# Moving table work between engines in the opening stage of a fused Fourier-mixing and maxout kernel

## The chip, the core and the metric

The kernel runs on one core of one Trainium2 chip. The metric is device time in microseconds of one execution; the figure for a kernel is the median of its runs. The core has a matrix engine (PE, with weight loads PEld), a vector engine (DVE), a scalar engine (ACT), GpSimd (POOL) and SyncE (SP), each with its own in-order queue. POOL and SP issue the transfers (DMA) here.

## The reference

For 8 batches of 3072 tokens by 256 features, the real part of a two-dimensional Fourier transform, then a feed-forward layer that takes the largest of three products:

```python
X = np.fft.fft(x, axis=1)          # x: (8, 3072, 256)
X = np.fft.fft(X, axis=2)
x = X.real.reshape(8 * 3072, 256)
h = np.maximum(np.maximum(x @ w1, x @ w2), x @ w3)   # w1, w2, w3: (256, 768)
out = h @ w_out                                      # w_out: (768, 256)
```

## The kernel before

**What it computes.** The transform along the tokens is done in two stages per batch (class `Mix`). Rows `a*96 + s` are loaded with `a` on partitions and `s` along the free dimension, the second 32 partitions holding the mirrored `s` (`load_x`); `mirror` copies features 255 to 129 into partitions 64 to 127, so that sums and differences of a pair come out of one product. Stage one (`s`, seven pieces) multiplies with a 32-point table `tab` and evicts into `tb`; for batch 0 a single DVE instruction, `t`, transposes `tb` into `yb` (later batches go through DRAM). Stage two (`k(which, g)`) multiplies `yb` with the tables `te_tab` (which 0) or `to_tab` (which 1), in three groups g of 512 columns, and evicts into `tE` and `tO`. The transform along the features is folded into the weights: `product` forms, for w2 and for w3, the feature transform times that weight less w1; `keep` evicts these banks into `g_all`, and `differ` makes `gd_all` from `g_all` for the mirrored tokens. What all three products share goes through `g1t` and `gw` straight to the output.

**Units.** A batch has 18 units: three blocks of 512 tokens by six chunks of 128 hidden columns. A unit's `begin` makes two sums on PE (four matmuls) and takes their maximum into `hp` (ACT writes `stmp`, DVE takes the maximum); its `finish` adds two matmuls with `gd_all` into the same banks and takes `hm` likewise. On PE the order is begin(g), finish(g-1), then what `plan` holds for that unit. The first bank of unit g is that of unit g-2, the second one too for even units, so a begin waits for ACT's `stmp` and DVE's `hm` of unit g-2. The last of the six chunks of a block is followed by the output products of that block (`l2_block`).

**The head.** All tables are made on the chip during batch 0's first two stages. For the stage-two tables POOL writes ramps into `kvec` (`ramp`, three iotas and three small ones). For each group of columns, `phase` turns the ramp into a phase (times `s_of`, plus `phi`, per partition), `turns` rounds it to whole turns by adding and taking away a large constant (two ACT operations into `q`), `wrap` takes the whole turns off (DVE), and `table(0)`, `table(1)`, `table(2)` write te_tab (sine), q (absolute value) and to_tab (sine of what is left), all on ACT. The feature tables `md_all` and `nmd_all` come from `vm` in the same way, with a period of 256. The third group's phase, turns and wrap are `angle(0)` and `angle(1)`, four DVE operations in units 1 and 2.

**Order.** The program's order is written by hand: every engine runs its instructions in the order in which the Python code issues them. Batch 0's x comes in four parts (`FIRST`, eight transfers issued by POOL), each followed by its `mirror`, DVE's for the block and ACT's for the first column (the fourth part's by DVE). `warm_up(n)` puts n matmuls on zeros where PE would else stand still. PSUM has three banks in `ps_f`, which banks of `product`, `k`, `g1t` and others pass through in turn; the five banks of `ps_s` serve stage one and then the units.

Lines of the profile that the change and the prediction speak of: L127 x loads, L134 and L138 mirrors, L150 iotas, L175 weight loads, L219 and L223 DVE or POOL arithmetic with scalars, L261 and L262 turns, L299 to L303 tables, L311 products, L325 keep, L332 differ, L341 g_all by `prep_first`, L371 g1t by `prep_second`, L405 and L413 stage-one evictions, L431 the transpose, L463 and L465 stage two and its evictions, L487, L488 and L494 unit matmuls, L500 stmp, L501 hp and hm, L637 warm-ups, L823 POOL's sums of later units.

Of the kernel before, what the change touches and what calls it, by code (L numbers as in the profile page):

```python
# [9 lines left out]
FP32 = mybir.dt.float32  # L10
# [3 lines left out]
AX = mybir.ActivationFunctionType  # L14
ALU = mybir.AluOpType
# [36 lines left out]
def kernel(  # L52
# [96 lines left out]
    def iota(t, pattern, base=0, cm=0):  # L149
        nc.gpsimd.iota(t, pattern, base=base, channel_multiplier=cm,  # L150
                       allow_small_or_imprecise_dtypes=True)
# [12 lines left out]
    for i in range(2):  # L164
        nc.vector.memset(xt[i][32:64, 0::48, :], 0.0)
    for c, (s0, s1) in enumerate(FIRST):
        for h in range(2):
            load_x(0, s0, s1, h)
        if c == 0:
            dvec = gen.tile([128, 128], FP32, tag="dvec")  # L170
            iota(dvec, [[1, 128]])

# [6 lines left out]
    kvec = gen.tile([128, NHALF + 1], FP32, tag="kvec")  # L179
    kv = kvec[:, 0:1440].rearrange("p (r j) -> p r j", j=96)  # L180

    def ramp(r):
        n = {0: 6, 6: 5, 11: 4}[r]
        iota(kv[:, r:r + n, :], [[1, n], [32, 96]], base=r + 1)

    load_w(0, 0, 128)
    ramp(0)
    load_w(1, 0, 128)
    ramp(6)
    load_w(2, 0, 128)  # L190
# [23 lines left out]
    def small(name):  # L214
        return gen.tile([128, 1], FP32, name=name, tag=name)
# [14 lines left out]
    scal(hflag, sidx, 32.0, ALU.is_ge)  # L230
    scal(alpha, sidx, -2.0, ALU.mult, 31.0, ALU.add)
# [27 lines left out]
    def turns(q, v, per):  # L259

        nc.scalar.activation(out=q, in_=v, func=AX.Identity, scale=1.0 / per, bias=rnd[:, 0:1])  # L261
        nc.scalar.activation(out=q, in_=q, func=AX.Identity, scale=1.0, bias=rnd[:, 1:2])  # L262

    turns(qm, vm, 256.0)
    phi, s_of = small("phi"), small("s_of")
    scal(phi, hflag, -768.0, ALU.mult, 1536.0, ALU.add)
    mad(s_of, hflag, -32.0, sidx)
    mad(s_of, s_of, 2.0, up)
    mirror(0, *FIRST[0])
# [3 lines left out]
    def phase(c0, c1):  # L273
        scal(kvec[:, c0:c1], kvec[:, c0:c1], s_of, ALU.mult, phi, ALU.add)
# [5 lines left out]
    turns(q[:, 0:512], kvec[:, 0:512], 3072.0)  # L280
    mad(vm, qm, -256.0, vm)
    nc.vector.tensor_copy(out=vm.rearrange("p (fc k c) -> p fc k c", fc=2, k=2)[:, :, :, 0],
                          in_=par.unsqueeze(1).to_broadcast([128, 2, 2]))
    phase(512, 1024)
    mirror(0, *FIRST[1])

    def angle(part, c0=1024, c1=NHALF + 1):
        cs = slice(c0, c1)
        if part == 0:
            phase(c0, c1)  # L290
            scal(q[:, cs], kvec[:, cs], 1.0 / 3072.0, ALU.mult, ROUND, ALU.add)
        else:
            scal(q[:, cs], q[:, cs], -ROUND, ALU.add, -3072.0, ALU.mult)
            nc.vector.tensor_tensor(out=kvec[:, cs], in0=kvec[:, cs], in1=q[:, cs], op=ALU.add)
# [65 lines left out]
    def prep_second():  # L360

        for jp in range(NJC // 2):
# [8 lines left out]
            nc.vector.tensor_copy(out=g1t[:, jp * 512:(jp + 1) * 512], in_=pst)  # L371
# [269 lines left out]
    m.s(0, pool=ps_s)  # L641
    m.s(1, pool=ps_s)
    warm_up(4)
    wrap(0, 512)
    mirror(0, *FIRST[2])
    nc.scalar.activation(out=md_all, in_=vm, func=AX.Sin, scale=float(2.0 * math.pi / 256.0))
    m.s(2, pool=ps_s)
    m.s(3, pool=ps_s, evict=dve)
# [6 lines left out]
    m.s(5, pool=ps_s)  # L655
    m.s(6, pool=ps_s, evict=dve)
# [3 lines left out]
    table(0, 0, 512)  # L660
# [3 lines left out]
    qs = q[:, 512:1024]  # L664
    scal(qs, kvec[:, 512:1024], 1.0 / 3072.0, ALU.mult, ROUND, ALU.add, eng=nc.gpsimd)
    scal(qs, qs, -ROUND, ALU.add, eng=nc.gpsimd)
    HALVES = ((0, 25), (25, NS))
    for (s0, s1) in HALVES:
        for h in range(2):
            load_x(1, s0, s1, h)  # L670
        if s0 == 0:
            nc.gpsimd.dma_start(out=wout_bf.rearrange("p (jc c) -> p jc c", jc=NJC),
                                in_=moe_w_out.rearrange("(jc p) c -> p jc c", jc=NJC))
    psg0 = products(ps_f, 0, 2, 0, 128)
    keep(psg0, 0, 2, 0, 128, nc.scalar.copy)
    table(1, 0, 512)
# [4 lines left out]
    warm_up(3)  # L681
    m.c(1, 7)
    m.k(0, 0, dve)
    m.k(1, 0)
    psg2 = products(ps_f, 1, 2, 128, 384)
    wrap(512, 1024)
    scal(dif, sgn, 1.0, ALU.subtract)
    differ(0, 2, 0, 128)
    keep(psg2, 1, 2, 128, 384, dve)
    table(1, 512, 1024)  # L690
    differ(0, 2, 128, 384)
    m.f()

    rows_f = gen.tile([128, 12 * B], FP32, tag="rows_f")
    iota(rows_f.rearrange("p (b t u) -> p b t u", t=4, u=3), [[S, B], [-4, 4], [-1025, 3]],
         base=S - 1, cm=-32)
    rows_v = rows_f.rearrange("p (b r) -> p b r", r=12)
    adj = gen.tile([128, 12], FP32, tag="adj")
    adv = adj.rearrange("p (t u) -> p t u", u=3)
    four = pidx.to_broadcast([128, 4])  # L700
    pool = nc.gpsimd
    for u in range(3):
        scal(adv[:, :, u], four, float(96 - 32 * u), ALU.is_ge, 3071.0, ALU.mult, eng=pool)
    low = gen.tile([128, 2], FP32, tag="low")
    scal(low[:, 0:1], pidx, 47.0, ALU.is_ge, 1520.0, ALU.mult, eng=pool)
    scal(low[:, 1:2], pidx, 95.0, ALU.is_ge, -511.0, ALU.mult, eng=pool)
    scal(low[:, 0:1], low[:, 0:1], 2031.0, ALU.add, eng=pool)
    pool.tensor_tensor(out=adj[:, 11:12], in0=low[:, 0:1], in1=low[:, 1:2], op=ALU.add)
    pool.tensor_tensor(out=rows_v, in0=rows_v,
                       in1=adj.unsqueeze(1).to_broadcast([128, B, 12]), op=ALU.add)  # L710
    pool.tensor_copy(rows_m, rows_f)
# [52 lines left out]
    for (u, fn) in ((0, lambda: table(2, 512, 1024)), (0, lambda: m.c(7, 16)),  # L764
                    (0, lambda: next(second)), (0, lambda: next(first)),
                    (1, lambda: m.k(1, 1)), (1, lambda: next(second)), (1, lambda: next(first)),
                    (1, lambda: table(0, 512, 1024)), (1, lambda: angle(0)),
# [152 lines left out]
```

## Time and profile before

| | |
|---|---|
| median of 3 runs | 400.74 us (398.99 to 402.38) |
| the profiled execution | 398.77 us, of which the span 396.9 |
| granted PE clock, mean over the span | 0.999 |
| PE busy, 0 to 10 us | 7.63 us |
| PE busy, 10 to 20 us | 6.30 us |
| PE busy, 20 to 30 us | 9.95 us |
| PE busy, 30 to 40 us | 7.77 us |
| PE busy, 40 to 50 us | 9.13 us |

The profile is one execution. Its span begins with the first instruction and ends with the last; the execution's own time is 1.9 us longer. A timeline row reads: start in us, duration in us, engine, source line, operation, what it writes and reads, partitions by elements and type, how often in a row, and in brackets how long the engine had been idle before it and what ended that. A row with xN stands for N equal instructions in a row, and its duration is from the first one's start to the last one's end. Consecutive instructions of one engine overlap by up to a tenth of a microsecond, so durations add up to a little more than the time they take. PE's busy time counts the warm-ups on zeros.

### The profile page before, as it was taken

What the parts mean: (1) busy time and instruction counts of PE and PEld (TensorE: products, weight loads), DVE (VectorE), ACT (ScalarE), POOL (GpSimd) and SP (SyncE); (2) the same over time, 40 slices, a digit from 0 to 9 for tenths busy, and PEclk for the clock granted to TensorE, in tenths of its full rate; (3) what the DMA queues carried; (4) which work ended last, traced back from release to release, by engine and by line L of the source; (5) the groups of instructions that cost most, each with busy time, mean ns of one, the idle gap of its engine ahead of it and who ended that gap; (6) DMA issues with size and microseconds to landing.
All of it is one profiled execution on the core that took longest, in us unless ns stands there. A gap on an engine that the chain in (4) does not pass through costs nothing.

```text
span 396.9 us, 8384 instructions
## 1 busy us (share of the span) xinstructions
PE 379.8 (96%) x2712; PEld 236.5 (60%) x2761; DVE 319.0 (80%) x534; ACT 261.9 (66%) x474; POOL 331.9 (84%) x430
## 2 busy tenths in 40 slices
PE   7697999999999999999999999999999999999994
PEld 2264566656665666656665666656665666666673
DVE  7897797887887887877887887877887887887982
ACT  3876789678767787578866788568766547444420
POOL 9983588879988899889988899889967898869993
PEclk9999999999999999999999999999999999999999
DMA  8999476494666876495666767395333553321234
GB/s 119 160 181 167 96 195 152 115 208 131 138 153 114 194 159 153 114 211 125 137 157 124 192 135 170 107 192 146 115 107 89 138 144 94 88 82 47 89 94 132
DMA packets 66901, 54.20 MB, mean 137 GB/s; under 512 B 32702, under 2 KB 62556, under 8 KB 66003
## 3 DMA queue, kind: packets, MB, share of 16 engines
q0 software_dynamic: 24368, 26.53, 35.2%
q1 hardware_dynamic: 41978, 26.72, 26.9%
q8 instruction: 21, 0.34, 0.4%
q10 hardware_dynamic: 512, 0.43, 0.3%
q14 instruction: 22, 0.18, 0.1%
HBM read 36.95 MB, written 30.81 MB: 171 GB/s over the span
## 4 chain that ended last, share of the span: by engine, by line
PE 83%; DVE 7%; ACT 4%; issue 3%; POOL 1%; DVEq 0%; POOLq 0%; ACTq 0%
PE po L510 30%; PE pse L494 12%; PE pse L487 8%; PE pse L488 6%; PE po L533 5%; PE pse L830 4%; PE d L816 3%; PE e L814 3%; PE pse L831 3%; PE ps L398 3%; PE ps L463 2%; PE pl L525 2%; ACT tb L402 1%; DVE yb L431 1%; ACT stmp L500 1%
## 5 line engine op out<-in xcount | busy, mean ns | idle before, releaser
L500 ACT ACTIVATE stmp<-pse 128x512 bf16<-128x512 f32 x150 | 89.5, 600 | 63.7 <-PE pse L494 50.3
L823 POOL TENSOR_TENSOR plus<-even,odd 128x512 bf16<-128x512 f32 x69 | 87.9, 1274 | 38.0 <-DVE even L819 27.8
L619 POOL DMA_INDIRECT out_dram<-ot,rows_m x92 | 102.5, 1114 | 17.8 <-issue 10.5
L823 POOL TENSOR_TENSOR minus<-even,odd 128x512 bf16<-128x512 f32 x69 | 87.7, 1270 | 0.0
L510 PE MATMUL po<-wout_bf,hp 128*128 128x256 bf16 x576 | 86.1, 273 | 0.4
L832 DVE SCALAR_TENSOR_TENSOR hp<-pse,plus 128x512 bf16<-128x512 f32 x69 | 47.6, 689 | 45.2 <-POOL plus L823 15.6
L510 PE MATMUL po<-wout_bf,hm 128*128 128x256 bf16 x576 | 78.6, 273 | 0.0
L510 PEld LDWEIGHTS <-hp 128*128 128x128 bf16 x576 | 56.4, 98 | 26.1
L494 PE MATMUL pse<-tO,gd_all 128*128 128x512 bf16 x218 | 70.8, 379 | 1.0
L510 PEld LDWEIGHTS <-hm 128*128 128x128 bf16 x576 | 56.4, 98 | 16.3
L538 DVE TENSOR_TENSOR ot<-po,even 128x512 f32<-128x512 f32 x92 | 62.7, 681 | 0.0
L487 PE MATMUL pse<-tE,g_all 128*128 128x512 bf16 x149 | 56.4, 379 | 3.3 <-DVE hm L501 1.6
L501 DVE TENSOR_TENSOR hp<-pse,stmp 128x512 bf16<-128x512 f32 x75 | 51.3, 684 | 9.4 <-ACT stmp L500 8.6
L501 DVE TENSOR_TENSOR hm<-pse,stmp 128x512 bf16<-128x512 f32 x75 | 51.5, 687 | 8.2 <-ACT stmp L500 3.5
L819 DVE SCALAR_TENSOR_TENSOR even<-vb,wcol,e 128x512 f32<-128x512 bf16 x69 | 50.9, 737 | 0.0
L488 PE MATMUL pse<-tO,g_all 128*128 128x512 bf16 x129 | 48.9, 379 | 0.1
L844 DVE SCALAR_TENSOR_TENSOR hm<-pse,minus 128x512 bf16<-128x512 f32 x69 | 47.1, 682 | 1.3 <-PE pse L488 0.7
L818 ACT ACTIVATE odd<-d 128x512 f32<-128x512 f32 x69 | 41.3, 599 | 6.4 <-issue 0.4
L134 ACT COPY xt<-xt 64x762 bf16<-64x762 bf16 (+1 forms) x48 | 40.2, 838 | 1.1
L494 PEld LDWEIGHTS <-gd_all 128*128 128x128 bf16 x219 | 21.3, 97 | 23.0 <-issue 5.0
L533 PE MATMUL po<-gw,tO 128*128 128x512 bf16 x85 | 32.3, 380 | 0.0
L402 ACT CAST tb<-ps 128x512 bf16<-128x512 f32 x40 | 21.6, 589 | 14.8 <-PE ps L398 14.0
(175 smaller groups left out, 478.0 us busy)
## 6 DMA issues: line engine op xcount, KB each, us to landing
xt<-in_x_dram POOLq DMA_DIRECT2D x14, 384.0 KB
out_dram<-ot SPq DMA_DIRECT2D x55, 96.0 KB
out_dram<-ot SPq DMA_DIRECT2D x64, 64.0 KB
db<-tb SPq DMA_DIRECT2D x21, 192.0 KB
vb<-vd SPq DMA_DIRECT2D x23, 128.0 KB
xt<-in_x_dram POOLq DMA_DIRECT2D x7, 400.0 KB
xt<-in_x_dram POOLq DMA_DIRECT2D x7, 368.0 KB
out_dram<-ot SPq DMA_DIRECT2D x62, 32.0 KB
```

The source lines that it names most:

```text
L487: nc.tensor.matmul(pse[:, 0:n], g_all[:, jc, 2 * i, :], te, start=True, stop=False)
L488: nc.tensor.matmul(pse[:, 0:n], g_all[:, jc, 2 * i + 1, :], to, start=False, stop=True)
L494: nc.tensor.matmul(pse, gd_all[:, jc, i, :], to, start=False, stop=True, skip_group_check=True)
L500: nc.scalar.activation(out=stmp[:, 0:n], in_=pses[0][:, 0:n], func=AX.Relu)
L501: nc.vector.tensor_tensor(out=dst, in0=src3, in1=stmp[:, 0:n], op=ALU.max)
L510: nc.tensor.matmul(po, hcols(jc), wout_bf[:, jc * 256:(jc + 1) * 256], start=False, stop=(jc == NJC - 1), skip_group_check=True)
L533: nc.tensor.matmul(po, to[:, cp], gw[:, 256:768], start=True, stop=True)
L538: nc.vector.tensor_tensor(out=ot.rearrange("p (h c) -> p h c", h=2), in0=po.rearrange("p (h c) -> p h c", h=2), in1=lin.unsqueeze(1).to_br ...
L619: stored(nc.gpsimd.indirect_dma_start(out, bass.IndirectOffsetOnAxis(ap=rows_m[0:128 - lo, at_row: at_row + 1], axis=0), ot[lo:128, 256:51 ...
L819: nc.vector.scalar_tensor_tensor(out=even3, in0=vb, scalar=wcol[:, jc:jc + 1], in1=e3, op0=ALU.mult, op1=ALU.add)
L823: nc.gpsimd.tensor_tensor(out=dst, in0=even3, in1=odd3, op=op)
L832: nc.vector.scalar_tensor_tensor(out=dst, in0=pse2, scalar=0.0, in1=sums[g][0], op0=ALU.max, op1=ALU.max)
```

## The change

What moves, by engine:

- POOL: the ramps of the first two groups go from between the first weight loads to between the parts of x. The two operations on `q` of the second group ahead of batch 1's loads go. `angle`, all four operations for the third group, comes to POOL behind `m.f`; the sums for the scatter indices (`rows`) go from there to unit 5.
- ACT: takes `phase` for two groups and `turns` for the second one; gives `turns` of vm to DVE. It evicts s3 and s6 of stage one, which DVE evicted, and DVE evicts s5, which ACT evicted. `md_all` comes two evictions later, `table(0)` and `table(1)` of early groups come earlier, the third group's `table(1)` moves from unit 3 to unit 2, and one of three g1t evictions comes from DVE.
- DVE: loses two phases, a product of vm, the third group's four operations, one eviction of g1t; takes the three operations of `_reduce` for vm; `wrap` of the second group moves ahead of the third mirror, `dif` ahead of the transpose.
- PE: the fourth product bank (psg2, eight matmuls) goes from behind stage two's first two pieces to ahead of them, and two warm-ups fewer stand there.

```diff
+    def ramp(r):
...
     for c, (s0, s1) in enumerate(FIRST):
         for h in range(2):
             load_x(0, s0, s1, h)
         if c == 0:
-            dvec = gen.tile([128, 128], FP32, tag="dvec")
             iota(dvec, [[1, 128]])
+        elif c < 3:
+            ramp((0, 6)[c - 1])
...
-    load_w(0, 0, 128)
-    ramp(0)
-    load_w(1, 0, 128)
-    ramp(6)
-    load_w(2, 0, 128)
+    for k in range(3):
+        load_w(k, 0, 128)
...
-    turns(qm, vm, 256.0)
...
     def phase(c0, c1):
-        scal(kvec[:, c0:c1], kvec[:, c0:c1], s_of, ALU.mult, phi, ALU.add)
+        nc.scalar.activation(out=kvec[:, c0:c1], in_=kvec[:, c0:c1], func=AX.Identity,
+                             scale=s_of, bias=phi)
...
     phase(0, 512)
-    turns(q[:, 0:512], kvec[:, 0:512], 3072.0)
-    mad(vm, qm, -256.0, vm)
+    turns(0, 512)
+    phase(512, 1024)
+    mirror(0, *FIRST[0])
+    turns(512, 1024)
+    _reduce(nc, vm, vm, qm, 256.0)
     nc.vector.tensor_copy(out=vm.rearrange("p (fc k c) -> p fc k c", fc=2, k=2)[:, :, :, 0],
                           in_=par.unsqueeze(1).to_broadcast([128, 2, 2]))
-    phase(512, 1024)
-    mirror(0, *FIRST[1])
+    wrap(0, 512)
...
+    def angle(c0=1024, c1=NHALF + 1):
+        v, t, pool = kvec[:, c0:c1], q[:, c0:c1], nc.gpsimd
+        scal(v, v, s_of, ALU.mult, phi, ALU.add, eng=pool)
+        scal(t, v, 1.0 / 3072.0, ALU.mult, ROUND, ALU.add, eng=pool)
+        scal(t, t, -ROUND, ALU.add, -3072.0, ALU.mult, eng=pool)
+        pool.tensor_tensor(out=v, in0=v, in1=t, op=ALU.add)
...
-            nc.vector.tensor_copy(out=g1t[:, jp * 512:(jp + 1) * 512], in_=pst)
+            (nc.scalar.copy if jp == 2 else nc.vector.tensor_copy)(
+                out=g1t[:, jp * 512:(jp + 1) * 512], in_=pst)
...
     m.s(0, pool=ps_s)
+    mirror(0, *FIRST[1])
     m.s(1, pool=ps_s)
     warm_up(4)
-    wrap(0, 512)
+    table(0, 0, 512)
+    wrap(512, 1024)
     mirror(0, *FIRST[2])
-    nc.scalar.activation(out=md_all, in_=vm, func=AX.Sin, scale=float(2.0 * math.pi / 256.0))
     m.s(2, pool=ps_s)
-    m.s(3, pool=ps_s, evict=dve)
+    m.s(3, pool=ps_s)
+    nc.scalar.activation(out=md_all, in_=vm, func=AX.Sin, scale=float(2.0 * math.pi / 256.0))
...
-    m.s(5, pool=ps_s)
-    m.s(6, pool=ps_s, evict=dve)
+    scal(dif, sgn, 1.0, ALU.subtract)
+    m.s(5, pool=ps_s, evict=dve)
+    m.s(6, pool=ps_s)
     m.t()
     warm_up(2)
     nc.scalar.activation(out=nmd_all, in_=vm, func=AX.Sin, scale=float(-2.0 * math.pi / 256.0))
-    table(0, 0, 512)
...
-    qs = q[:, 512:1024]
-    scal(qs, kvec[:, 512:1024], 1.0 / 3072.0, ALU.mult, ROUND, ALU.add, eng=nc.gpsimd)
-    scal(qs, qs, -ROUND, ALU.add, eng=nc.gpsimd)
...
     psg0 = products(ps_f, 0, 2, 0, 128)
+    table(1, 0, 512)
     keep(psg0, 0, 2, 0, 128, nc.scalar.copy)
-    table(1, 0, 512)
     table(2, 0, 512)
     psg1 = products(ps_f, 0, 1, 128, 384)
     m.x0(x0s)
     keep(psg1, 0, 1, 128, 384, nc.scalar.copy)
-    warm_up(3)
+    psg2 = products(ps_f, 1, 2, 128, 384)
+    table(1, 512, 1024)
     m.c(1, 7)
+    warm_up(1)
     m.k(0, 0, dve)
     m.k(1, 0)
-    psg2 = products(ps_f, 1, 2, 128, 384)
-    wrap(512, 1024)
-    scal(dif, sgn, 1.0, ALU.subtract)
     differ(0, 2, 0, 128)
     keep(psg2, 1, 2, 128, 384, dve)
-    table(1, 512, 1024)
     differ(0, 2, 128, 384)
     m.f()
+    angle()
+
+    def rows():
...
-                    (1, lambda: table(0, 512, 1024)), (1, lambda: angle(0)),
+                    (1, lambda: table(0, 512, 1024)),
...
-                    (2, lambda: next(second)), (2, lambda: next(first)), (2, lambda: angle(1)),
+                    (2, lambda: next(second)), (2, lambda: next(first)), (2, lambda: table(1)),
                     (3, lambda: m.c(16, RI)), (3, lambda: m.c(0, 1)),
-                    (3, lambda: table(1)), (3, lambda: table(2)), (3, lambda: table(0)),
+                    (3, lambda: table(2)), (3, lambda: table(0)), (5, rows),
```

The lines of `rows` are those that stood behind `m.f` before, now in a function. `phi` and `s_of` are computed a little earlier on DVE.

## The prediction

> **What bounds the kernel now.** I read the page first (busy time, slices), then busy time by stage, then the head engine by engine in order of time.
>
> ```profile
> span 396.9 us, 8384 instructions
> PE 379.8 (96%) x2712; PEld 236.5 (60%) x2761; DVE 319.0 (80%) x534; ACT 261.9 (66%) x474; POOL 331.9 (84%) x430
> ```
> ```profile
> 0.00:19.90 19.90, 13.83 (x69) 5.67 (x70) 16.79 (x54) 12.14 (x24) 18.65 (x40) 1.00 1.00 139
> 19.90:36.43 16.53, 14.25 (x111) 8.37 (x114) 14.03 (x26) 12.77 (x28) 12.73 (x28) 1.00 1.10 168
> 45.00:390.00 345.00, 341.95 (x2453) 216.43 (x2496) 280.78 (x441) 231.17 (x411) 297.76 (x360) 1.00 0.59 135
> ```
>
> The last three rows are stretches: length, then busy us of PE, PEld, DVE, ACT, POOL, then PE clock and DMA. From 45 to 390 us PE is busy 341.95 of 345: that part runs at PE's pace and keeps its length, whatever happens in the head. So the change, which moves nothing behind unit 5 of batch 0, is worth what it takes off the start of that PE-bound run. In the head PE waits: 2.28 of the 16.53 us after 19.9, and before 19.9 much of its work is warm-up on zeros.
>
> Who it waits for, by the timeline:
>
> ```profile
> 7.66 0.81 DVE L134 COPY xt<-xt 64x2032 bf16<-64x2032 bf16 x1
> 8.49 0.99 DVE L219 TENSOR_SCALAR kvec<-kvec,s_of,phi 128x512 f32<-128x512 f32 x1
> 9.41 0.67 DVE L223 SCALAR_TENSOR_TENSOR vm<-qm,vm 128x512 f32<-128x512 f32 x1
> 10.12 0.60 DVE L282 COPY vm<-par 128x4 f32<-128x4 f32 x1
> 10.19 0.78 DVE L219 TENSOR_SCALAR kvec<-kvec,s_of,phi 128x512 f32<-128x512 f32 x1
> ...
> 13.16 0.69 DVE L405 CAST tb<-ps 128x512 bf16<-128x512 f32 x1
> 13.87 0.48 DVE L134 COPY xt<-xt 64x1143 bf16<-64x1143 bf16 x1
> ...
> 16.07 3.78 DVE L431 STREAM_TRANSPOSE yb<-tb 128x2048 uint32<-128x2048 uint32 x1 [0.52 <-ACT tb L405]
> 20.34 0.69 DVE L465 CAST tE<-ps 128x512 bf16<-128x512 f32 x1 [0.50 <-PE ps L463]
> 20.95 0.68 DVE L223 SCALAR_TENSOR_TENSOR kvec<-q,kvec 128x512 f32<-128x512 f32 x1
> ```
> ```profile
> 15.14 0.59 ACT L405 CAST tb<-ps 128x512 bf16<-128x512 f32 x1 [0.88 <-PE ps L408]
> ```
> ```profile
> 21.33 0.38 PE L487 MATMUL pse<-tE,g_all 128*128 128x512 bf16 x1
> 31.27 0.38 PE L487 MATMUL pse<-tE,g_all 128*128 128x512 bf16 x1 [0.47 <-ACT stmp L500]
> 33.42 0.38 PE L487 MATMUL pse<-tE,g_all 128*128 128x512 bf16 x1 [1.56 <-DVE hm L501]
> 35.14 0.81 PE L487 MATMUL pse<-tE,g_all 128*128 128x512 bf16 x2
> ```
>
> DVE has no gap from 7.66 to the fourth mirror at 13.87. That mirror releases the last stage-one matmuls, ACT evicts one of them until 15.73, and 0.34 later the transpose starts; stage two follows it. After the transpose DVE is again without a gap until about 33.4, and PE's largest stall (1.56, at 33.42) ends on DVE's hm. Two DVE queues in a row, then, set when PE's even run begins.
>
> **Part 1: up to the transpose.** From DVE's queue between 7.66 and 13.87 the change takes the two phases (0.99 and 0.78), the product of vm (0.67) and the eviction of s3 (0.69): 3.13. It puts in vm's whole reduction (three operations) and the second wrap, which moves here. The nearest rows of these:
>
> ```profile
> 27.58 0.43 DVE L219 TENSOR_SCALAR q<-kvec 128x513 f32<-128x513 f32 x1
> 31.04 0.41 DVE L219 TENSOR_SCALAR q<-q 128x513 f32<-128x513 f32 x1
> 31.48 0.70 DVE L294 TENSOR_TENSOR kvec<-kvec,q 128x513 f32<-128x513 f32 x1
> ```
>
> Reduction 0.43 + 0.41 + 0.70 = 1.54, wrap 0.68, in all 2.22: DVE could reach the fourth mirror at 13.87 - 0.91 = 12.96. But the data must be there. No view gives its landing; the packets do:
>
> ```profile
> DMA packets 333, 0.09 MB, mean 172 GB/s; under 512 B 310, under 2 KB 333, under 8 KB 333
> ```
>
> That is 12.0 to 12.5 us: 310 of 333 packets are already the short ones of the first weight loads, which stand behind x in the queue, so nearly all of x is through; 13.87 is the upper bound, since the mirror started without waiting. I take 13.25, near the lower end: 0.62 gained. The two ramps now stand between x's issues:
>
> ```profile
> 3.10 3.35 POOL L127 DMA_DIRECT2D xt<-in_x_dram  x6
> 7.14 0.73 POOL L150 IOTA kvec<- 128x576 f32 x1
> 8.62 0.58 POOL L150 IOTA kvec<- 128x480 f32 x1
> ```
>
> They push the issue of the fourth part 0.73 + 0.58 = 1.31 later, to end at 7.76. I cost that at nothing, because the transfers lag the issues by some 6 us (issued by 6.45, through after 12) and are fed from a backlog; if they followed the issue one for one, landing would be up to 1.31 later and this part's gain gone (rival 2). From there the chain is as before but for the last eviction, now DVE's at 0.69 instead of ACT's at 0.59: +0.10. Gain of part 1: 0.62 - 0.10 = 0.52, say **0.5**; bounds 0.8 (landing never waited for) and 0 (the reduction held up by POOL by 0.6, as the 128x4 copy at 10.12 shows such a hold). ACT takes two phases and four turns (six at 0.72, 4.3 us) from about 5.2 us on, where it now waits for DVE; its evictions of s2 and s3, the table md, s4 and s6 (four at 0.54 from start to start, 0.28) then need 2.4 us from 12.1 and end before DVE's eviction of s5 (14.5 to 15.2). The new transpose start is 16.07 - 0.5 = 15.57, its end 19.35.
>
> **Part 2: the first unit.** The fourth product bank (eight matmuls, 0.88) leaves the place between stage two and unit 0 and goes under the transpose:
>
> ```profile
> 18.25 0.59 PE L637 MATMUL warm<-zero 128*128 128x512 bf16 x2
> 20.45 0.38 PE L311 MATMUL psg<-w_bf,md_all 128*128 128x256 bf16 x2
> ```
>
> Cover: PE has only warm-ups from 18.25 to 19.90; 18.25 + 0.88 is 19.1, and one warm-up of 0.2 still fits. Unit 0 then starts as soon as tE is evicted: that took 20.34 + 0.69 - 19.85 = 1.18 after the transpose, against 21.33 - 19.85 = 1.48 before. Gain **0.3** (0 to 0.3); the rest of the 0.88 becomes slack on PE, which is not the late one here.
>
> **Part 3: units 0 to 5.** DVE loses the wrap (0.68), the third group's four operations (0.68 by the row below, 0.43, 0.41, 0.70) and one g1t (0.68): 3.6 us of the 13 between 20.3 and 33.4.
>
> ```profile
> 26.87 0.68 DVE L219 TENSOR_SCALAR kvec<-kvec,s_of,phi 128x513 f32<-128x513 f32 x1
> 29.59 0.68 DVE L371 CAST g1t<-pst 128x512 bf16<-128x512 f32 x1
> 29.44 0.48 ACT L341 CAST g_all<-psg 128x384 bf16<-128x384 f32 x1 [0.90 <-PE psg L311]
> 29.88 1.34 ACT L500 ACTIVATE stmp<-pse 128x512 bf16<-128x512 f32 x2
> 32.21 0.63 ACT L301 ACTIVATE q<-kvec 128x513 f32<-128x513 f32 x1 [0.82 <-DVE kvec L294]
> ```
>
> What is late next is ACT. It gains that g1t (0.59) and does the third group's Abs (0.63) ahead of unit 3's two stmp instead of behind them. Of this g1t fits ACT's idle time before 29.44 (0.9), Abs does not. Counted from the transpose's end: unit 3's stmp at 10.35 and 10.9 to 11.5 (before, 29.88 - 19.85 = 10.03 and to 11.4), hm behind it to 12.3, so unit 4's second pair starts at 12.3 against 33.42 - 19.85 = 13.57. Then ACT does the last two tables (0.65 and 0.55 from start to start) and two stmp (0.53 each), and unit 5 starts at 14.1 against 35.14 - 19.85 = 15.29: **1.2** less, the 0.3 of part 2 in it. From there PE's work is the same.
>
> POOL: angle is four operations. The rows nearest to them:
>
> ```profile
> 16.60 0.62 POOL L219 TENSOR_SCALAR q<-kvec 128x512 f32<-128x512 f32 x1
> 17.31 1.52 POOL L219 TENSOR_SCALAR q<-q 128x512 f32<-128x512 f32 x1
> 43.35 1.27 POOL L823 TENSOR_TENSOR plus<-even,odd 128x512 bf16<-128x512 f32 x1 [9.64 <-ACT tb L402]
> ```
>
> Three at 0.62 and one at 1.27 make 3.1, four at 1.52 make 6.1. With the first two rows' 2.1 us gone ahead of batch 1's loads, POOL is free when the transpose ends; m.f's copies and memsets (1.7 us) come first, so angle starts at about 21.4 and ends between 24.5 and 27.5; ACT asks for it at 19.35 + 9.8 = 29.1. It is hidden as long as it takes under 7.7 us; beyond that each us costs one. The loads of batch 1 go out 2 us earlier, and the index sums (3.7 us) end by 37.5, ahead of the first plus at 43.35 and of any scatter: nothing.
>
> **The sum.** 0.5 + 1.2 = 1.7. The profiled execution took 398.77 us (span 396.9 and 1.9 around it): 397.1 after. The median of the runs shown is 400.74, 2 above it: 400.74 - 1.7 = **399.0**.
>
> **Rivals.**
> 1. More comes off. The transpose's 3.78 lies beside POOL's 0.62 and 1.52; one of like form takes 2.5 times the other. If that 0.9 is mutual hindrance, the transpose loses 0.9 as well: 2.6 off, 398.1. For it: the two rows; against: the first of the two ran under the same transpose and was short. 0.13.
> 2. Nothing to speak of comes off. The load sets the fourth mirror (part 1 gives 0) and ACT is held by g1t and Abs together (1.2 less 0.6 to 1.2): 0 to 0.6 off, 400.4. 0.17.
> 3. Slower: POOL's angle holds up DVE. One row shows how:
>
> ```profile
> 26.60 0.34 DVE L332 TENSOR_SCALAR gd_all<-g_all,dif 128x384 bf16<-128x384 bf16 x1
> 29.52 1.45 POOL L134 COPY xt<-xt 64x1524 bf16<-64x1524 bf16 x1
> 30.18 0.93 DVE L332 TENSOR_SCALAR gd_all<-g_all,dif 128x384 bf16<-128x384 bf16 x1
> ```
>
> The same operation took 0.34, and 0.93 when it met a POOL copy, ending at 31.11 as the copy had ended (30.97). Four such products stand in units 0 to 2, where POOL now runs four long operations in a row. If three lose a whole POOL operation each (1.52), DVE gets 4.6 us back for 3.6 taken off; it is then again the late one, unit 4 starts 1.0 later after the transpose, and with part 1's 0.5 the kernel is 0.5 slower, 401.2. It decides from 3.6 + 0.5 = 4.1 us lost on DVE. Against: POOL ran the index sums and mirrors in the same stretch before, and each product has some 0.7 us of room ahead of the next hp, which waits for ACT. 0.08.
> The Trainium skill, page SBUF — State Buffer, section "Who interferes with whom", says that a DVE instruction in a 2-port mode and a GpSimd instruction exclude each other for the whole length of the one that came first, and advises against running them together on a path that matters; by that rule this rival holds. The trace agrees in kind (0.34 against 0.93).
>
> The forecast itself has 0.62. That the change does not do what it says I leave out: the order of instructions in the changed program shows every move.
>
> **How the numbers follow.** The cases with weight span 398.1 to 400.4. Medians of so few runs move too (the runs shown go from 398.99 to 402.38), by an estimated 1.1: 397.0 to 401.5, which takes in rival 3. About 1% (4 us) is what can be told from no change. No case reaches it; it takes run-to-run drift or a hidden larger stall. Faster by over 1%: 0.06; within: 0.90; slower: 0.04.
>
> **What would show it.** Right: the transpose starts near 15.6 and ends near 19.4; PE's stall on hm before unit 4's second pair falls from 1.56 to under 0.5; unit 5's first matmul is at about 33.4. Wrong: a wait on DMA ahead of the third or fourth mirror beyond 13.5; ACT's third Abs released by POOL; a product for gd_all of over 0.9; or the 45 to 390 stretch with PE under 99%, which would give the gain back.

## The result and the profile after

The changed kernel took 397.22 us (median of 6 runs, 396.32 to 397.90), the kernel before 400.84 (6 runs, 398.99 to 402.38): a ratio of 0.991, interval 0.9882 to 0.9937, 3.6 us less. The forecast was 399.0. The profiled execution of the changed kernel took 397.9, its slowest of six, so the two profiles lie closer together than the two medians.

First the busy times by stretch, from the transpose's end (19.79) to unit 5, from there to the fourth output tile, and the long run (columns as in the prediction):

```profile
19.79:33.50 13.71, 12.25 (x98) 7.07 (x99) 10.70 (x18) 11.20 (x25) 12.35 (x24) 1.00 1.14 173
33.50:54.60 21.10, 20.34 (x153) 12.08 (x150) 17.26 (x30) 15.24 (x29) 11.80 (x18) 1.00 0.71 142
45.00:390.00 345.00, 343.95 (x2496) 216.48 (x2496) 279.60 (x439) 230.53 (x409) 296.60 (x360) 1.00 0.59 135
```

The long run is as tight as before, and from unit 5 to the fourth output tile both kernels take 21.1, so what was gained lies ahead of unit 5. DVE up to the transpose, by the timeline:

```profile
7.85 1.00 DVE L134 COPY xt<-xt 64x2032 bf16<-64x2032 bf16 x1
8.88 0.43 DVE L23 TENSOR_SCALAR qm<-vm 128x512 f32<-128x512 f32 x1
9.35 0.86 DVE L25 TENSOR_SCALAR qm<-qm 128x512 f32<-128x512 f32 x1
10.24 0.69 DVE L27 TENSOR_TENSOR vm<-vm,qm 128x512 f32<-128x512 f32 x1
...
13.30 0.92 DVE L134 COPY xt<-xt 64x1016 bf16<-64x1016 bf16 x2
...
15.23 0.69 DVE L406 CAST tb<-ps 128x512 bf16<-128x512 f32 x1 [0.27 <-PE ps L409]
16.04 3.75 DVE L432 STREAM_TRANSPOSE yb<-tb 128x2048 uint32<-128x2048 uint32 x1
```

The transpose starts at 16.04, against 16.07 before. The row at 13.30 is the third and the fourth mirror together; the fourth, of 0.48 before, begins at about 13.30 + 0.92 - 0.48 = 13.74, against 13.87. The head has gained nothing in this pair of executions. PE after the transpose:

```profile
21.03 0.38 PE L488 MATMUL pse<-tE,g_all 128*128 128x512 bf16 x1 [0.48 <-DVE tE L466]
31.18 0.38 PE L488 MATMUL pse<-tE,g_all 128*128 128x512 bf16 x1 [0.68 <-ACT stmp L501]
32.01 0.38 PE L488 MATMUL pse<-tE,g_all 128*128 128x512 bf16 x1 [0.24 <-DVE hm L502]
33.50 0.38 PE L488 MATMUL pse<-tE,g_all 128*128 128x512 bf16 x1
```

The rows are unit 0, the two pairs of unit 4, and unit 5, which before stood at 21.33, 31.27, 33.42 and 35.14. PE's stall on hm fell from 1.56 to 0.24. POOL's angle, with the copies for batch 1 behind it:

```profile
21.64 0.78 POOL L218 TENSOR_SCALAR kvec<-kvec,s_of,phi 128x513 f32<-128x513 f32 x1
22.51 0.62 POOL L218 TENSOR_SCALAR q<-kvec 128x513 f32<-128x513 f32 x1
23.22 0.62 POOL L218 TENSOR_SCALAR q<-q 128x513 f32<-128x513 f32 x1
23.92 1.27 POOL L294 TENSOR_TENSOR kvec<-kvec,q 128x513 f32<-128x513 f32 x1
25.50 1.55 POOL L134 COPY xt<-xt 64x1651 bf16<-64x1651 bf16 x1 [0.31 <-DMA xt<-in_x_dram]
```

It ends at 25.19. ACT needs it only at the row of 29.52 below, which follows g_all without a wait:

```profile
29.14 0.48 ACT L341 CAST g_all<-psg 128x384 bf16<-128x384 f32 x1 [0.16 <-PE psg L311]
29.52 0.64 ACT L301 ACTIVATE q<-kvec 128x513 f32<-128x513 f32 x1
30.05 1.07 ACT L501 ACTIVATE stmp<-pse 128x512 bf16<-128x512 f32 x2
31.00 0.29 ACT L457 COPY yb<-x0s 128x1 bf16<-128x1 bf16 x2
31.18 0.75 ACT L303 ACTIVATE to_tab<-q,half_pi 128x513 bf16<-128x513 f32 x1
31.80 0.64 ACT L299 ACTIVATE te_tab<-kvec 128x513 bf16<-128x513 f32 x1
32.32 1.13 ACT L501 ACTIVATE stmp<-pse 128x512 bf16<-128x512 f32 x2
```

Behind unit 5 the gain of 1.64 keeps until stage two of batch 1, where ACT waits for a transfer. The fifth output tile is DVE's row for `ot` at 61.56, against 61.99 before, so in this pair 1.2 of the 1.64 was lost there. ACT's wait, before and after:

```profile
59.96 0.23 ACT L452 CAST yb<-psx 128x16 bf16<-128x16 f32 x1 [1.14 <-DMA yb<-db]
```
```profile
59.53 0.23 ACT L453 CAST yb<-psx 128x16 bf16<-128x16 f32 x1 [2.34 <-DMA out_dram<-ot]
```

Two questions follow. Where do 3.6 us come from, if the path to unit 5 became 1.64 shorter and part of that is gone again at 60 us? And which of the three parts did it?

### The profile page after: what moved, and what is told of

It is laid out like the page before. It is cut to its first block, busy times and chain, and to the rows that moved or that the text cites. A ratio compares the mean times of both kernels' runs of the same rounds, so it can differ in the third digit from the quotient of the medians.

```text
span 396.1 us, 8431 instructions
## 1 busy us (share of the span) xinstructions
PE 380.5 (96%) x2759; PEld 235.8 (60%) x2759; DVE 316.5 (80%) x528; ACT 263.7 (67%) x478; POOL 332.0 (84%) x432
## 4 chain that ended last, share of the span: by engine, by line
PE 88%; DMA 4%; DVE 2%; ACT 2%; POOL 1%; issue 1%; DVEq 0%; POOLq 0%; SPq 0%
PE po L511 30%; PE pse L495 12%; PE pse L488 8%; PE pse L489 8%; PE po L534 5%; PE pse L831 4%; PE pse L832 4%; PE e L815 4%; PE d L817 4%; PE ps L399 3%; PE ps L464 3%; PE pl L526 2%; DMA yb<-db 2%; DMA xt<-in_x_dram 2%; DVE yb L432 1%
## 5 line engine op out<-in xcount | busy, mean ns | idle before, releaser
L511 PEld LDWEIGHTS <-hm 128*128 128x128 bf16 x576 | 56.3, 98 | 16.4
L489 PE MATMUL pse<-tO,g_all 128*128 128x512 bf16 x150 | 56.8, 379 | 0.0
L534 PE MATMUL po<-gw,tO 128*128 128x512 bf16 x92 | 34.9, 380 | 0.0
```

What stands on the lines that cost most here:

```text
L489: nc.tensor.matmul(pse[:, 0:n], g_all[:, jc, 2 * i + 1, :], to, start=False, stop=True)
L511: nc.tensor.matmul(po, hcols(jc), wout_bf[:, jc * 256:(jc + 1) * 256], start=False, stop=(jc == NJC - 1), skip_group_check=True)
L534: nc.tensor.matmul(po, to[:, cp], gw[:, 256:768], start=True, stop=True)
```

## The experiments

Every kernel was run beside the kernel before. Its ratio to that one is given with its interval.

**The same kernels again.** No edit.

> The kernel before, unchanged, for a second profile and the spread. Its six times lie from 398.99 to 402.38 us, while the profiled execution took 398.77. Theory: the head is the same in every execution (unit 5's first matmul at 35.1 +- 0.2 us), and what an execution takes beyond 398.8 is lost later, at the place where batch 1's stage two waits for yb's way through DRAM (50 to 62 us). Rival: executions differ in the head, or evenly over the span. Time 400 to 401.5, ratio 1.00.

> The changed kernel, unchanged, for a second profile. In the first one the head was 1.64 us shorter (unit 5's first matmul at 33.50 against 35.14) and 1.2 us of it were lost again at 59 to 61 us, ACT waiting 2.34 us ahead of its copy into yb. Theory: the head repeats (33.5 +- 0.2), the loss at 59 us varies between 0 and 2 us. Rival: the loss is fixed, since the transfers set it. Ratio 0.989 to 0.994.

The kernel before: 400.06 (12 runs), ratio 0.9998 (0.9981 to 1.0015). The changed one: 397.18 (6 runs), ratio 0.9925 (0.9899 to 0.9951). So the difference repeats, at about 3.0. But neither head does: unit 5's first matmul comes at 35.68 in the kernel before, not at 35.1, and at 34.44 in the changed one, not at 33.5. Both theories fall on that point. What these traces have and the first two profiles have not is a drop of PE's clock. First the kernel before (this profiled execution took 400.59, not 398.77), its PE rows and two windows that follow each other:

```profile
33.73 0.38 PE L487 MATMUL pse<-tE,g_all 128*128 128x512 bf16 x1 [1.43 <-DVE hm L501]
...
35.68 0.59 PE L487 MATMUL pse<-tE,g_all 128*128 128x512 bf16 x1
```
```profile
31.00:34.40 3.40, 1.50 (x8) 0.50 (x6) 2.65 (x5) 2.62 (x7) 3.02 (x6) 1.00 0.67 119
34.40:37.80 3.40, 3.40 (x26) 1.77 (x25) 1.43 (x3) 2.74 (x7) 0.00 (x0) 0.51 1.32 211
```

The seventh number of a window is the granted PE clock. PE worked 1.50 of 3.40 us around its stall, and for the next 3.4 us it ran at half clock: unit 5's matmul takes 0.59 where it took 0.38. From there to the fourth output tile (57.85) this execution needs 22.17; the first profile needed 56.24 - 35.14 = 21.10. The window costs 1.07.

The same trace has another such window in stage one:

```profile
13.90:17.30 3.40, 3.11 (x15) 1.22 (x14) 2.27 (x7) 2.23 (x5) 3.31 (x9) 0.51 1.16 157
```

The changed kernel's second trace has one too, from 13.0 to 16.4 at a clock of 0.50, and there the price can be read, because DVE's queue is the same as in the first profile to within 0.04 as far as the mirrors (13.34 against 13.30):

```profile
13.34 0.92 DVE L134 COPY xt<-xt 64x1016 bf16<-64x1016 bf16 x2
...
16.16 0.69 DVE L406 CAST tb<-ps 128x512 bf16<-128x512 f32 x1 [1.17 <-PE ps L399]
16.96 3.75 DVE L432 STREAM_TRANSPOSE yb<-tb 128x2048 uint32<-128x2048 uint32 x1
```

PE's stage-one matmuls end later, and the transpose starts at 16.96 instead of 16.04. So half-clock windows ahead of the transpose come in both kernels, and the change does not take them away. The traces of two later versions of the changed kernel (ramps back, loads later) have one as well.

**Part 1 undone.** The kernel before, its head up to the transpose as it was, with the changed kernel's psg2, angle, rows and g1t (the first three shown):

```diff
+    psg2 = products(ps_f, 1, 2, 128, 384)
     m.c(1, 7)
...
     m.f()
+    angle()
...
-                    (1, lambda: table(0, 512, 1024)), (1, lambda: angle(0)),
+                    (1, lambda: table(0, 512, 1024)),
```

> Part 1 undone: ramps, phases, turns, evictions and wraps as before; the fourth product bank ahead of stage two, angle on POOL, index sums in unit 5, one g1t by ACT as after. Theory (part 1 is worth almost nothing: the transpose began at 16.04 against 16.07): unit 5's first matmul at 33.5 to 34.0, time within 0.5 us of the changed kernel, ratio 0.991 to 0.994. Rival (part 1 gives the 2 us by which the medians differ more than the head does, by issuing batch 1's loads 2.5 us earlier): head the same, but a ratio of 0.996.

397.41 (7 runs), ratio 0.9933 (0.991 to 0.9956): 0.2 above the changed kernel, less than the intervals tell apart, with unit 5 at 33.74. The theory holds: the head's rearrangement is worth little or nothing.

**Part 3 undone.** The changed kernel with the angle on DVE, g1t on DVE, and `rows` behind `m.f`:

```diff
-    angle()
+    rows()
...
-                    (1, lambda: table(0, 512, 1024)),
+                    (1, lambda: table(0, 512, 1024)), (1, lambda: angle(0)),
...
-                    (2, lambda: next(second)), (2, lambda: next(first)), (2, lambda: table(1)),
+                    (2, lambda: next(second)), (2, lambda: next(first)), (2, lambda: angle(1)),
```

> Part 3 undone: angle's four operations on DVE in units 1 and 2, the third Abs in unit 3, all g1t by DVE, index sums behind m.f; part 1 and the bank as after. Theory (DVE's queue set the stall before unit 4's second pair): that stall comes back to over 1 us, unit 5's first matmul at 34.6 to 35.0, ratio 0.996 to 0.999. Rival (the bank and the wrap that left the place behind the transpose did it): unit 5's first matmul at 33.5 to 34.0, ratio 0.991 to 0.994.

400.10 (12 runs), ratio 1.0002 (0.9979 to 1.0025): all of the gain is gone, though parts 1 and 2 are still in. That is more than the theory had: unit 5 came at 35.86, not at 34.6 to 35.0. DVE's row and POOL's:

```profile
27.10 1.76 DVE L218 TENSOR_SCALAR kvec<-kvec,s_of,phi 128x513 f32<-128x513 f32 x1
```
```profile
27.12 1.45 POOL L134 COPY xt<-xt 64x1524 bf16<-64x1524 bf16 x1
```

The angle's first operation, 0.68 in the first profile, met a POOL copy. So this run does not give the price of part 3 alone: it also has a collision that the first profile of the kernel before lacks, and the next run has two.

**The angle alone back on DVE**, with g1t left on ACT and `rows` in unit 5 (the same edit without the first two lines):

> The changed kernel with the third group's angle back on DVE, in units 1 and 2, and its table(1) back in unit 3; the g1t eviction stays on ACT and the index sums stay in unit 5. Theory (the angle is what DVE could not carry): DVE gets its 2.2 us back (0.68 + 0.43 + 0.41 + 0.70), PE again waits for DVE in units 3 or 4 for over 0.8 in one place, unit 5's first matmul comes 1.0 to 2.0 later after the transpose's end than in the changed kernel (13.7), and the median is 398.5 to 400.0, ratio 0.995 to 0.999. Rival (the g1t and the index sums carry it): the median stays at 397.0 to 397.6.

399.81 (12 runs), ratio 0.9986 (0.9967 to 1.0004). The median is where the theory put it. The stall is larger than it said: unit 5's first matmul comes 16.85 after the transpose's end, 3.1 later than in the changed kernel, for 2.2 of DVE's work. DVE's rows, POOL's, PE's, and a window:

```profile
26.23 1.87 DVE L218 TENSOR_SCALAR kvec<-kvec,s_of,phi 128x513 f32<-128x513 f32 x1
28.14 1.71 DVE L218 TENSOR_SCALAR q<-kvec 128x513 f32<-128x513 f32 x1
```
```profile
26.27 1.55 POOL L134 COPY xt<-xt 64x1651 bf16<-64x1651 bf16 x1 [4.75 <-DMA xt<-in_x_dram]
...
28.11 1.45 POOL L134 COPY xt<-xt 64x1524 bf16<-64x1524 bf16 x1
```
```profile
31.56 0.39 PE L490 MATMUL pse<-tE,g_all 128*128 128x512 bf16 x1 [2.35 <-DVE g_all L343]
```
```profile
33.40:34.40 1.00, 1.00 (x3) 0.26 (x2) 0.61 (x2) 0.97 (x3) 0.81 (x4) 0.50 0.66 90
```

The same two operations took 0.68 and 0.43 in the kernel before. Here each meets a POOL copy and ends 0.3 after it; the copies are about as long as before (1.61 and 1.45 there). The last row, a window of 1 us, has PE at half clock behind its stall of 2.35, which is in the 3.1 too. With nothing ahead of them POOL's copies start as soon as batch 1's x is there, just when DVE does the angle.

**g1t alone back on DVE:**

```diff
-            (nc.scalar.copy if jp == 2 else nc.vector.tensor_copy)(
-                out=g1t[:, jp * 512:(jp + 1) * 512], in_=pst)
+            nc.vector.tensor_copy(out=g1t[:, jp * 512:(jp + 1) * 512], in_=pst)
```

> The changed kernel with the third g1t eviction back on DVE. Theory (with the angle gone DVE and ACT are about even): within 0.5 of the changed kernel, 397.0 to 397.7, with unit 4's stalls moved by less than 0.4. Rival A (DVE still the late one): unit 4's second pair waits 0.5 to 0.7 longer for hm, 397.7 to 398.2. Rival B (ACT is the late one, as the prediction had it): PE's wait for stmp of 0.68 at unit 4 falls by about 0.5, 396.6 to 396.9.

397.34 (6 runs), ratio 0.9929 (0.9909 to 0.9949). Unit 5 stands 13.72 after the transpose, as in the changed kernel (13.71). This eviction is free on either engine; both rivals fall.

**The index sums ahead of the angle on POOL:**

```diff
-    angle()
...
+    rows()
+    angle()
...
-                    (3, lambda: table(2)), (3, lambda: table(0)), (5, rows),
+                    (3, lambda: table(2)), (3, lambda: table(0)),
```

> The changed kernel with the index sums back in front of the angle on POOL, so that the angle starts about 3.7 us later, near 25.3 instead of 21.6, and ends near 29.0. Theory (the angle is hidden as long as it ends before ACT asks for it, at 29.5): 397.0 to 397.6, ACT's third Abs not released by POOL or by under 0.2. Rival (POOL's long operations beside DVE's products and sums of units 2 and 3, or a late angle, cost time): ACT's third Abs waits for POOL, or a DVE operation in units 2 and 3 is longer by over 0.5, and the median is 397.8 to 399.0.

397.09 (6 runs), ratio 0.9931 (0.991 to 0.9952). The angle ran from 25.49 to 29.04 and ACT, whose third Abs starts at 29.07, did not wait for it, so it is hidden, if only just, even 3.9 later. But the rival's sign is there too. DVE's rows, then POOL's and PE's:

```profile
29.05 1.74 DVE L332 TENSOR_SCALAR gd_all<-g_all,dif 128x384 bf16<-128x384 bf16 x1 [0.59 <-ACT g_all L341]
30.72 0.67 DVE L502 TENSOR_TENSOR hp<-pse,stmp 128x512 bf16<-128x512 f32 x1
```
```profile
29.10 1.55 POOL L134 COPY xt<-xt 64x1651 bf16<-64x1651 bf16 x1
...
30.74 1.45 POOL L134 COPY xt<-xt 64x1524 bf16<-64x1524 bf16 x1
```
```profile
32.04 0.38 PE L488 MATMUL pse<-tE,g_all 128*128 128x512 bf16 x1 [0.73 <-DVE hm L502]
```

A product of 0.34 us became 1.74 beside a POOL copy, and unit 5 came at 14.34 after the transpose instead of 13.71. The median doesn't show the 0.63; this trace's transpose was also early (15.45). `hp`, which reads PSUM, took its usual 0.67 beside the next copy.

**The ramps back between the weight loads**, on the changed kernel:

```diff
-        elif c < 3:
-            ramp((0, 6)[c - 1])
...
-    for k in range(3):
-        load_w(k, 0, 128)
+    load_w(0, 0, 128)
+    ramp(0)
+    load_w(1, 0, 128)
+    ramp(6)
+    load_w(2, 0, 128)
```

> The changed kernel with the two ramps back between the first weight loads. In the changed kernel DVE's small operations of the angle tables took longer while POOL ran the ramps (0.62 for 0.38, 0.64 for 0.24, 0.51 for 0.23) and the first mirror began at 7.85, not at the 7.55 that was worked out. Theory (POOL's iotas hold those DVE operations): they go back to 0.38, 0.24 and 0.23 and the first mirror begins at 7.4 to 7.6; ACT's first phase waits for its ramp until about 7.9 and the transpose begins later than 16.04, by up to 1 us; ratio 0.991 to 0.995. Rival (the operations were long for another reason): their durations stay, the first mirror begins at 7.8 or later.

398.26 (7 runs), ratio 0.9949 (0.9931 to 0.9968): 1.0 above the changed kernel. ACT's row shows the price:

```profile
7.89 0.81 ACT L267 ACTIVATE kvec<-kvec,phi,s_of 128x512 f32<-128x512 f32 x1 [2.47 <-POOL kvec L150]
```

Phases and turns are now ACT's, ahead of its evictions, so a late ramp makes all of stage one late: the transpose starts at 17.29. This trace also has a half-clock window, from 11.8 to 15.2, which may be part of the 17.29; it does not set the median, for the seven executions lie within 0.23 of each other at mean clocks from 0.991 to 1.000. The theory's other sign came too: DVE's small operations of the angle tables took 0.20, 0.26 and 0.23 where they had taken 0.62, 0.64 and 0.51, and the first mirror began at 7.55. So POOL's ramps do hold them; that costs 0.3 at the first mirror, and the late ramps cost more. The ramps' new place brings nothing over the kernel before; it pays for the phases' new engine.

**No warm-ups ahead of s5:**

```diff
     m.s(4, pool=ps_s)
-    warm_up(2)
```

> The changed kernel without the two matmuls on zeros between s4 and s5 of stage one. In its profile s5's data was ready at 14.39 and PE came to it at 14.78, behind those two. Theory (they stand on the path to the transpose): s5 starts at 14.45 to 14.55, the transpose at 15.7, 0.3 earlier; the head is 0.3 shorter, the time lower by 0 to 0.5 (a wait for yb at 59 us may take it). Rival (they keep the clock up): the granted clock falls to 0.992 or less in most executions and the time rises by 0.5 to 1.

397.20 (6 runs), ratio 0.9925 (0.9904 to 0.9947): nothing. Its DVE row says why:

```profile
13.98 0.54 DVE L134 COPY xt<-xt 64x1143 bf16<-64x1143 bf16 x1 [0.45 <-DMA xt<-in_x_dram]
```

Here DVE was early, and the fourth part of x was not there. So s5 came at 14.68, no earlier than its data, and this trace doesn't tell what the two matmuls cost; the median says that leaving them out gains nothing. The rival's sign did not come either: the mean clock was 0.992 or less in two of six.

**Batch 3's first loads later**, in case they hold up the transfer that ACT waits for near 60 us:

```diff
-                at(b - 3, (9 + (b == 3), 11, 18, 19)[ch], lambda b=b, ch=ch: fetch(b, ch))
+                at(b - 3, ((13, 14, 18, 19) if b == 3 else (9, 11, 18, 19))[ch], lambda b=b, ch=ch: fetch(b, ch))
```

> The changed kernel with the first two loads of batch 3's x moved from units 10 and 11 of batch 0 (issued at 54.0 and 58.6 us) to units 13 and 14. Theory (those loads share the transfers with yb's way back from DRAM, for which ACT waited 2.34 us at 59 us): that wait falls below 1.3 us, the third to fourth output tile (54.6 to 61.55 us) take under 6.0, time lower by 0.3 to 0.8, ratio to before 0.989 to 0.992. Rival (yb's transfers are slow by themselves, or because of the output's): wait of 1.3 to 2.4 as in the profiles so far, time unchanged, ratio 0.991 to 0.994.

397.32 (6 runs), ratio 0.9924 (0.9903 to 0.9946). The wait was 1.43 in this trace; it was 2.34 and 1.30 in the two of the unedited kernel, so it lies within what it was without the edit, and the time is unchanged: the rival holds. In its head DVE waited for x as well:

```profile
13.79 0.48 DVE L134 COPY xt<-xt 64x1143 bf16<-64x1143 bf16 x1 [0.36 <-DMA xt<-in_x_dram]
```

**Zeros in PE's stall**, on the kernel before: six matmuls, then three, between unit 4's two pairs.

```diff
         for (pse, i) in ((pse2, 0), (pse3, 1)):
+            if i and fill:
+                idle = ps_f.tile([128, 512], FP32, name="idle", tag="ps")
+                for _ in range(fill):
+                    nc.tensor.matmul(idle, zero[:, 0:128], zero, start=True, stop=True)
```

> The kernel before with six matmuls on zeros put into PE's stall in the middle of unit 4's begin (31.9 to 33.4 us, 6 x 0.216 = 1.3 us), on a bank of ps_f that is free there; nothing that DVE or ACT does changes. So far executions of before with a mean granted clock of 0.994 or less have a median of 400.5 and those at 0.996 or more 399.1, and a second profile of before showed the clock at half for 3.4 us from 34.4 us on. Theory (the stall lets the clock drop, and that is the part of the gain that the path does not explain): executions at 0.996 or more go from 14 of 36 to a clear majority, the median falls to 399.0 to 399.5, ratio 0.996 to 0.998, and unit 5's first matmul stays at 35.1. Rival (the clock drops for other reasons): clocks and time as before, ratio 0.999 to 1.001.

> The kernel before with three zero matmuls instead of six in PE's stall in unit 4 (three take 0.64 us of the 1.43 to 1.56 there), so that they end before the maximum that PE waits for and cost nothing on the path. Theory (the drops of the granted clock behind that stall make the slower executions): most executions at a clock of 0.996 or more, median 399.0 to 399.5, ratio 0.996 to 0.998. Rival (the clock only goes along with something else): the median stays at 400.0 to 400.6 although the clock is up. Third: three are too few to keep the clock, and clock and median stay as before.

Six: 399.86 (12 runs), ratio 0.9989 (0.9975 to 1.0003). Three: 399.52 (12 runs), ratio 0.9986 (0.9970 to 1.0003). The mean clock was 0.996 or more in 11 and in 9 of 12 executions, against 30 of 76 executions of the kernel before. In the same two rounds it was 16 of 40. The medians fell by 0.8 and 0.9, the ratios say 0.4 and 0.6, and neither interval leaves out 1. Six were also too many: in that trace unit 4's second pair started as the sixth ended. That a filled stall keeps the clock up is well supported; what it is worth is not settled. The trace with three showed another cause. DVE's row and POOL's:

```profile
30.41 1.82 DVE L294 TENSOR_TENSOR kvec<-kvec,q 128x513 f32<-128x513 f32 x1
```
```profile
29.99 1.69 POOL L134 COPY xt<-xt 64x1524 bf16<-64x1524 bf16 x1
```

The angle's last operation, 0.70 in the first profile, took 1.82, and unit 4's second pair came 14.23 after the transpose instead of 13.57. The zeros had ended long before it. The trace with six has such a row as well:

```profile
28.31 1.67 DVE L219 TENSOR_SCALAR q<-kvec 128x513 f32<-128x513 f32 x1
```
```profile
28.11 1.59 POOL L134 COPY xt<-xt 64x1651 bf16<-64x1651 bf16 x1 [0.22 <-POOL rows_m L715]
```

This operation took 0.43 in the first profile. So both paths are longer for a reason of their own, whatever the zeros do.

## Why the prediction was right, and where it was not

The traces side by side, each number from that trace's rows of the kinds named above (us; the output tiles are DVE's rows for `ot`):

| kernel | transpose starts | its end to unit 5 | unit 5 to 4th tile | 4th to 5th tile |
|---|---|---|---|---|
| before, first profile | 16.07 | 15.29 | 21.10 | 5.75 |
| before, again | 16.49 | 15.44 | 22.17 | 6.22 |
| before, six zeros | 16.96 | 15.81 | 21.10 | 6.40 |
| before, three zeros | 15.50 | 15.94 | 21.11 | 6.33 |
| part 3 undone | 15.81 | 16.30 | 21.11 | 6.17 |
| angle on DVE | 15.72 | 16.85 | 21.11 | 6.08 |
| changed, first profile | 16.04 | 13.71 | 21.11 | 6.95 |
| changed, again | 16.96 | 13.73 | 21.10 | 5.91 |
| part 1 undone | 16.19 | 13.76 | 21.11 | 5.96 |
| g1t on DVE | 15.90 | 13.72 | 21.10 | 6.36 |
| sums first | 15.45 | 14.34 | 21.11 | 6.07 |
| ramps back | 17.29 | 13.71 | 21.11 | 6.02 |
| no warm-ups | 15.93 | 13.72 | 21.11 | 6.11 |
| loads later | 16.30 | 13.71 | 21.11 | 6.04 |

From the fifth tile to the end of the span each of the 14 traces takes 334.5 to 334.9, so what tells the traces apart lies in these four columns.

The direction and the carrier were right: DVE's angle held PE, and POOL can do it at no cost that shows on the path. By steps:

- **Part 1, 0.5: wrong.** 0.03 between the first profiles, 0.2 by the medians with part 1 undone. In the first profile of the changed kernel DVE got to the fourth mirror only near 13.74: the first mirror took 1.00 and the reduction 0.43 + 0.86 + 0.69 where I had 0.81 and 1.54. In five other traces with the same head DVE was early (13.22 to 13.53, where I had 12.96) and waited for x, to 13.49, 13.79, 13.81, 13.84 and 13.98, mostly about as late as the kernel before (13.87). So the step that failed is the reading of x's landing, 12.0 to 12.5, and "I take 13.25, near the lower end" with it. In the version without warm-ups 284 of 307 packets from 12.5 to 13.0 were under 512 B, the share that I had taken for x nearly through, and the mirror still waited until 13.98. Rival 2's first half, that the load sets the fourth mirror, held. Whether the ramps between x's issues pushed the load, which I cost at nothing, is not shown: no trace with the old head waited there, and in one of them (three zeros) x was in by 13.47. Leaving out the traces with a half-clock window in stage one, the transpose starts at 15.50 to 16.96 with the old head (four traces) and at 15.45 to 16.04 with the new one (six): a gain of a few tenths is possible, but these are too few to tell.
- **Part 2, 0.3: right.** Unit 0 starts 21.03 - 19.79 = 1.24 after the transpose, against 1.48 before.
- **Part 3, 1.2 with part 2 in it: right in mechanism, too small.** Unit 4's second pair stands at 12.22 (I had 12.3), unit 5 at 13.71 (I had 14.1): 1.58. The term that was off is the one for ACT's last two tables: I placed them behind unit 4's second pair, but ACT does both by 32.4, while PE's second pair runs.
- **POOL's angle: right.** 3.55 us from 21.64, inside my 3.1 to 6.1, and over four us early.
- **Rival 3: its mechanism is real, its price too high.** The changed kernel has a product of 0.91 (over my sign of 0.9) and the version with the sums first one of 1.74, costing 0.63. With part 1 undone two products took 1.12 and 1.16 and cost nothing (13.76). It never came to three that cost. The Trainium skill (SBUF — State Buffer, section "Who interferes with whom") says that a DVE instruction with one SBUF input outside the 2-port modes never meets GpSimd, while one with two SBUF inputs meets a GpSimd instruction that reads SBUF, as 2-port ones do with any; the traces agree, with `hp` at 0.67 and the `kvec` sum at 1.82 beside POOL copies. What I overlooked is that the rule speaks against the order of before still more: its angle stands on DVE right beside those copies.
- **Rivals 1 and 2.** Rival 1's mechanism fell: with no POOL arithmetic beside it the transpose took 3.75, against 3.78. Of rival 2 the first half held, as said; the second fell, since g1t on ACT or on DVE made no difference (13.71 and 13.72).
- **The sum.** 0.5 + 1.2 happens to be 1.7, and the two profiles have 1.64 at unit 5, with the terms the other way round. The step that failed is the last: "The median of the runs shown is 400.74, 2 above it: 400.74 - 1.7 = 399.0". The measured 397.22 lies below every case that I gave a weight (398.1 to 400.4); only the 1.1 added for the scatter of medians takes it into the range. I took what lay between the profiled execution and the median for an offset that the change would leave alone.
- **That offset.** Two things that made other executions of the kernel before longer are now known, and both sit in the stretch that the change relieves: an angle that meets a POOL copy (15.94 with three zeros, in place of 15.29; in the 15.81 with six, the zeros have a part), and a half-clock window behind PE's stall (22.17 in place of 21.10). No trace with the angle on POOL has either between the transpose and the fourth tile, save the product in the version with the sums first; from 31.0 to 34.4 PE is busy 2.7 to 3.1 of 3.4 us in the six traces with the angle on POOL whose transpose starts by 16.3, and 1.6 in the first profile of the kernel before. A third thing, a half-clock window in stage one, comes in both kernels, so that part of the offset did stay. Against the profiled execution the sum had given 397.1, close to the measured median, but in part by luck: between the two profiled executions only 0.9 came off. The loss of 1.2 at 60 us was not the change's: the last column runs from 5.75 to 6.40 with the angle on DVE (mean 6.16) and from 5.91 to 6.95 with it on POOL (mean 6.18), and the first pair of profiles had the two ends.

What stays open is how the 1.4 to 2.0 beyond the path's 1.58 divide, since one trace a kernel tells no frequency. The mean clocks give a rough division: among executions at 0.996 or more the kernel before has a median of 399.26 (30 of 76) and the changed kernel one of 396.86 (9 of 12), 2.4 apart. So some 0.8 beyond the path comes without a lower clock, for which the collisions are a candidate, and the rest goes with the clock. None of the variants is faster than the changed kernel by more than the intervals.

## What to carry to other kernels

Work out a gain against the profiled execution, then ask why the other executions are slower than it: if the reason is in the stretch that the change relieves, the gain on the median is larger; what slows both kernels stays. Before an operation between SBUF tiles is put on DVE or POOL, look at what the other engine does in the same microseconds, for what starts a POOL copy (a transfer in the version with the angle on DVE, POOL's own index sums in the kernel before) does not keep step with DVE's queue: in the kernel before and its two versions with zeros the first copy starts 7.4 to 9.1 us after the transpose's end. Ramps that feed an engine early in its queue belong early in the queue of the engine that makes them; here their late place cost 1.0.

## What the runs showed that was not expected

Six half-clock windows of 3.4 us, at a clock of 0.50 or 0.51, stand in five of the traces: two in the second one of the kernel before (from 13.93 and 34.44), one each with the angle on DVE (32.33), in the changed kernel's second (13.00), with the ramps back (11.77) and with the loads later (13.95). In the 3.41 us ahead of them PE was busy 1.70, 1.51, 1.06, 1.47, 0.51 and 1.53 us. Stretches as slack stand in the first profiles without such a window behind them (1.57 of 3.40 from 31.0 in the kernel before, 1.50 of 3.40 from 9.2 in the changed one). The two windows of one trace start 20.5 us apart, six times 3.42, as they would on a fixed grid; that the place of a stall on such a grid decides is not shown beyond this. The Trainium skill (TensorE: Matmul & The Clock Gate, section "What's actually happening") has the clock halved in free-running windows of 3413 ns by how busy PE was, after an idle one; length and halving agree, but here the stretches ahead were 15 to 50% busy, not idle. The 30 executions of the kernel before with a mean clock of 0.996 or more had a median of 399.26, the other 46 one of 400.63.

Six DVE operations between SBUF tiles (five of the angle's, one product for gd_all) took 1.67 to 1.87 in place of 0.34 to 0.70 when they met a POOL copy, and the copy was at most 0.24 longer than its 1.45. The kernel before's product of 0.93 met its copy half-way through.
